# A sinkhorn attention and FFN kernel on one core: half-width FFN1 tiles taken in pairs, and new orders for the five engine queues

## The chip, the core and the metric

The kernel runs on one core of a Trainium2 chip. The metric is the device time of one execution in microseconds (us); the figure for a kernel is the median of several runs. The core has a matrix engine (PE; its weight loads are listed apart as PEld), a vector engine (DVE), a scalar engine (ACT), a general engine (POOL) and SP, which here does nothing but issue transfers. Each engine works through a queue of its own in order, and waits on semaphores for what other engines and transfers deliver. PSUM, where PE leaves its sums, has eight banks of 2 KB a partition.

## The reference

An attention in blocks, whose output goes through a two-layer feed-forward network (FFN):

```python
# q, k, v: (4 batches, 8 heads, 768 tokens, 64); sort_net: (4, 8, 8, 8); n_blocks 8, block 96
P = sort_net
for _ in range(5):
    P = P - np.max(P, axis=-1, keepdims=True)
    P = np.exp(P)
    P = P / (np.sum(P, axis=-1, keepdims=True) + 1e-09)
    P = P / (np.sum(P, axis=-2, keepdims=True) + 1e-09)
k_sorted = np.einsum('bhij,bhjcd->bhicd', P, k_b)      # blocks of keys, mixed by P
v_sorted = np.einsum('bhij,bhjcd->bhicd', P, v_b)
scores = scale * np.matmul(q_b, k_sb.transpose(0, 1, 2, 4, 3))
attn = softmax(scores)
x = (attn @ v_sb), heads joined: (3072 tokens, 512)
h = x @ w_in                                           # 512 -> 2048
g = np.maximum(h, 0.0) + alpha * np.minimum(h, 0.0)
out = g @ w_out                                        # 2048 -> 512
```

## The kernel before

**The work.** There are 4 batches (here 0 to 3) of 8 blocks, so 32 groups of 96 tokens, numbered 0 to 31; a group is one block of one batch with all its heads. For each group `attention` multiplies Q and sorted K (L758 and L762 for the row maxima and, for batch 0, L778 and L789 once more with the maximum taken off), takes the maximum on DVE (L770), the exponential on ACT (L797, L809), multiplies with the sorted values (L820, the sum of a row among its columns), divides (L825, L828) and turns the result so that features lie on the partitions (`xT`; by PE at L842 for batches 0 and 1, by a DMA transpose at L835 later). From batch 1 on (the code's `far`) the exponentials `Esb` are themselves turned by a DMA transpose that SP issues (L802, `ET`), and so are Q's rows (`turn_q`, L441: `QN` to `QT`).

The FFN takes `xT` in chunks of tokens. The first two chunks have 192 tokens (two groups each), the other seven 384. `ffn1` (L852) makes one tile, 128 of the 2048 hidden features of one chunk: four matmuls (L861) into one PSUM bank, a Relu of the negative on ACT into one of three buffers `t1` (L868), and one step on DVE (L871) that multiplies it by 1 - alpha and adds h from the bank: the leaky Relu, written to `hT`. There are 16 tiles a chunk: 32 of 192 tokens, 112 of 384. `ffn2` (L882) makes 128 tokens of the output from `hT` and `w_out`: 16 matmuls in four quarters (L895), a copy to a staging buffer (L904, done by the helper of L397) and a store that SP issues (L906). The last 128 tokens are made in two halves.

**Before the FFN.** The loads go through POOL: q, k and v of batch 0; `w_in` in four quarters (L933); the keys `KS` (L457, by `load_k`), queries `QN` (L430, by `load_q`, one load a head, eight a batch) and values `VST` (L475, by `load_v`) of batches 1 to 3; `w_out` in two halves (L938). Meanwhile DVE and ACT run the five sinkhorn rounds on a 32 x 64 matrix, `spread0` (L577) spreads P of batch 0 over the partitions, and `prep_q` (L640), `prep_k0` (L657) and `prep_v` (L721) turn and sort Q, K and V of batch 0 on PE. Until `w_out` is loaded its memory holds three selection matrices that L577 reads; the load of `w_out`'s first half must wait for L577. For later batches POOL copies keys and values into zero-padded blocks (`conv_k`, L676, to `KSz`; `conv_v`, to `VDz`; the memsets of L496 and L502 clear such blocks), and PE sorts them against `BDM` and `BDV` (`prep_k` L688, `prep_v` L716); DVE or ACT copy the results out of PSUM (L397) to `KT` and `VS`.

**What sets the order.** Every step is a node of a graph (`_Graph`), added with what it reads and writes. A table `ORDER` gives, for each of the five queues, the numbers of the nodes in the order in which that engine runs them; a number is a node's place in the order of creation, so that the same step has another number when nodes are added or dropped ahead of it. A node that may run on ACT or DVE (`EITHER`: copies from PSUM) runs on the one whose row holds it. An entry with a point, as `12.1`, is a filler: 12 matmuls of the identity into bank 1 (L1018), whose result nobody reads. A string `BANKS` gives the PSUM banks. `place` adds the waits for a bank's earlier holder, and `emit` puts semaphore waits where a node needs something of another engine or of a transfer. The durations and priorities that the nodes carry (`dur`, `prio`) are not used for the order, which is the table's alone:

```python
for x in order[e].split():
    if "." in x:
        k, b = x.split(".")
        op = _Op(("pe",), filler(int(k), int(b)), 0, 0, None, len(self.ops))
...
    else:
        op = self.ops[int(x)]
    op.eng, op.pos = e, len(row)
    row.append(op)
```

PE's first entry is a burst of 180 small matmuls (L917). A load or a transpose counts as issued when its engine has handed it over; its landing is a semaphore of its own.

Of the kernel before, what the change touches and what calls it, by code (L numbers as in the profile page):

```python
# [7 lines left out]
AP = bass.AP  # L8
# [9 lines left out]
DFF = 2048  # L18
# [4 lines left out]
XR = 1536  # L23
# [19 lines left out]
        733 675 673 904 905 909 935 910 934 801 800 831 771 772""",  # L43
    "sync": """
# [3 lines left out]
        1137 1109 1077 1065 1117 1212 1167 1191 1245 1233 1239 1251""",  # L48
    "pe": """
# [17 lines left out]
        1242 1231 1243 1246 1236 1237 1247 1248 1249""",  # L67
    "act": """
# [989 lines left out]
```

## Time and profile before

| | |
|---|---|
| median of 3 runs | 235.33 us (235.2 to 235.4) |
| the profiled execution | 234.94 us |
| its span (first to last instruction) | 233.2 us |
| PE busy | 222.9 us, 96% |
| DVE, ACT, POOL busy | 172.1, 156.4, 104.3 us |
| granted PE clock | 1.00 |
| moved by DMA | 28.99 MB, mean 124 GB/s |
| FFN1 on PE (L861) | 576 matmuls, 96.0 us |
| FFN2 on PE (L895) | 89.6 us in the 375 records that the trace holds |

All views come from one profiled execution. A group of instructions has the columns line, engine, operation, output <- inputs with their shape, count, then after the bar the busy time in us, the mean of one in ns, and the engine's idle time just before them with what ended most of it. In the view of waits a row names who waited, for what it waited, the idle us, the count and the longest. In the timeline a row has the start, the duration, the engine, the line, output <- inputs and how many instructions it holds. The windows view has a row for each stretch: start, end and length, then the busy time and count of each engine in the order PE, PEld, DVE, ACT, POOL, the granted clock, the mean share of the 16 DMA engines that is busy (over 1 where more than 16 transfers' worth overlaps) and GB/s. A DMA row gives the queue, the count, the KB of one and the us from issue to landing. Some matmul records can be missing from a trace.

### The profile page before, as it was taken

What the parts mean: (1) busy time and instruction counts of PE and PEld (TensorE: products, weight loads), DVE (VectorE), ACT (ScalarE), POOL (GpSimd) and SP (SyncE); (2) the same over time, 40 slices, a digit from 0 to 9 for tenths busy, and PEclk for the clock granted to TensorE, in tenths of its full rate; (3) what the DMA queues carried; (4) which work ended last, traced back from release to release, by engine and by line L of the source; (5) the groups of instructions that cost most, each with busy time, mean ns of one, the idle gap of its engine ahead of it and who ended that gap; (6) DMA issues with size and microseconds to landing.
All of it is one profiled execution on the core that took longest, in us unless ns stands there. A gap on an engine that the chain in (4) does not pass through costs nothing.

```text
span 233.2 us, 6024 instructions
## 1 busy us (share of the span) xinstructions
PE 222.9 (96%) x2389; PEld 143.2 (61%) x2414; DVE 172.1 (74%) x353; ACT 156.4 (67%) x431; POOL 104.3 (45%) x148
## 2 busy tenths in 40 slices
PE   7679899999999999999999999999999999999995
PEld 4369787776566666665656656556565556555553
DVE  6776889898889878988798687956769368644650
ACT  5316789878598979797858787568847864341711
POOL 7904949998999996268499570000000000000000
PEclk9999999999999999999999999999999999999999
DMA  5999999999997999996697935565481534201113
GB/s 83 220 208 210 214 191 191 218 138 140 100 109 126 154 96 170 176 195 76 131 151 83 87 67 111 129 155 148 26 214 34 70 72 143 61 0 45 45 48 135
DMA packets 63036, 28.99 MB, mean 124 GB/s; under 512 B 55312, under 2 KB 58144, under 8 KB 63008
## 3 DMA queue, kind: packets, MB, share of 16 engines
q0 software_dynamic: 23680, 13.63, 43.6%
q1 hardware_dynamic: 39328, 14.97, 32.2%
q8 instruction: 19, 0.31, 0.6%
q14 instruction: 9, 0.07, 0.1%
HBM read 27.28 MB, written 6.29 MB: 144 GB/s over the span
## 4 chain that ended last, share of the span: by engine, by line
PE 86%; DVE 8%; ACT 3%; issue 2%; POOL 0%; POOLq 0%
PE ps L895 34%; PE ps L861 34%; PE ps L758 4%; PE ps L820 3%; PE ps L721 3%; PE ps L716 2%; DVE hT L871 2%; PE ps L688 2%; PE ps L789 1%; PE ps L842 1%; DVE nm L770 1%; PE ps L778 1%; PE ps L762 1%; ACT ET L809 1%; ACT t L868 1%
## 5 line engine op out<-in xcount | busy, mean ns | idle before, releaser
L871 DVE SCALAR_TENSOR_TENSOR hT<-t,omaT,ps 128x384 bf16<-128x384 f32 (+1 forms) x144 | 76.9, 561 | 29.5 <-ACT t L868 28.6
L861 PE MATMUL ps<-xT,w_in_bf 128*128 128x384 bf16 (+1 forms) x576 | 96.0, 308 | 0.0
L895 PE MATMUL ps<-w_out_bf,hT 128*128 128x512 bf16 (+1 forms) x375 | 89.6, 370 | 1.3
L868 ACT ACTIVATE t<-ps 128x384 f32<-128x384 f32 (+1 forms) x144 | 61.3, 456 | 39.0 <-PE ps L861 29.6
L861 PEld LDWEIGHTS ps<-xT,w_in_bf 128*128 128x128 bf16 x576 | 51.9, 98 | 29.1 <-DVE hT L871 0.8
L895 PEld LDWEIGHTS ps<-w_out_bf,hT 128*128 128x128 bf16 x400 | 37.2, 98 | 31.8
L797 ACT ACTIVATE Esb<-ps,nf 96x96 bf16<-96x96 f32 x192 | 46.3, 346 | 4.9 <-DVE nf L770 4.9
L397 POOL COPY VDz<-VST 64x384 bf16<-64x384 bf16 x40 | 33.9, 848 | 7.4 <-PE ps L716 5.0
L676 POOL COPY KSz<-KS 64x512 bf16<-64x512 bf16 x36 | 22.2, 618 | 14.5 <-DMA KS<-in_k_dram 9.4
L770 DVE TENSOR_REDUCE nf<-ps 96x8 f32<-96x768 f32 x24 | 22.7, 947 | 4.0 <-PE ps L758 2.1
L828 DVE TENSOR_TENSOR xq<-ps,rec 96x512 bf16<-96x512 f32 x32 | 21.7, 682 | 0.6
L430 POOL DMA_DIRECT2D QN<-in_q_dram x24 | 20.1, 841 | 4.3 <-DVE hT L871 4.3
L397 ACT ACTIVATE KT<-ps 64x512 bf16<-64x512 f32 (+1 forms) x28 | 16.5, 589 | 6.0 <-PE ps L657 3.3
L397 ACT ACTIVATE VS<-ps 112x512 bf16<-112x512 f32 (+1 forms) x20 | 13.8, 691 | 4.6 <-PE ps L721 4.1
L397 ACT ACTIVATE outstg<-ps 128x512 f32<-128x512 f32 (+1 forms) x13 | 7.5, 580 | 10.0 <-PE ps L895 10.0
L820 PEld LDWEIGHTS ps<-VS,ET 112*128 112x128 bf16 (+1 forms) x256 | 11.1, 98 | 3.8 <-DVE hT L871 0.9
L820 PE MATMUL ps<-VS,ET 112*128 112x65 bf16 (+1 forms) x256 | 13.0, 194 | 0.2 <-DVE hT L871 0.2
L397 DVE COPY outstg<-ps 128x512 f32<-128x512 f32 (+1 forms) x12 | 7.9, 662 | 6.8 <-PE ps L895 6.8
L758 PE MATMUL ps<-KT,QT 128*96 128x192 bf16 x96 | 12.0, 247 | 0.4 <-DVE hT L871 0.4
L758 PEld LDWEIGHTS ps<-KT,QT 128*96 128x96 bf16 x96 | 9.2, 123 | 3.6 <-ACT VS L397 0.9
L825 DVE RECIPROCAL rec<-ps 96x8 f32<-96x8 f32 x32 | 6.3, 199 | 6.4 <-PE ps L820 6.2
L716 PEld LDWEIGHTS ps<-BDV,VDz 128*128 128x128 bf16 x192 | 8.4, 98 | 3.3 <-DVE VS L397 0.4
(96 smaller groups left out, 181.7 us busy)
## 6 DMA issues: line engine op xcount, KB each, us to landing
out_dram<-outstg SPq DMA_DIRECT2D x23, 256.0 KB, 2.4
KS<-in_k_dram POOLq DMA_DIRECT2D x3, 768.0 KB, 12.3
QN<-in_q_dram POOLq DMA_DIRECT2D x24, 96.0 KB, 3.9
w_in_bf<-in_moe_w_in_dram POOLq DMA_DIRECT2D x4, 512.0 KB, 11.5
w_out_bf<-in_moe_w_out_dram POOLq DMA_DIRECT2D x2, 1024.0 KB, 10.8
VST<-in_v_dram POOLq DMA_DIRECT2D x4, 384.0 KB, 8.3
hT<-in_q_dram POOLq DMA_DIRECT2D x1, 768.0 KB, 7.0
hT<-in_v_dram POOLq DMA_DIRECT2D x2, 384.0 KB, 10.4
```

Of the source, the lines that this page charges most:

```text
L397: return e.activation(o, i, ACTF.Copy) if e is nc.scalar else e.tensor_copy(o, i)
L430: G.add(POOL, lambda e, h=h: e.dma_start(AP(QN[b % 2], h % 4 * 128 + h // 4 * 64, [[3072, 128], [512, 6], [1, 64]]), AP(q.tensor, b * HB + ...
L676: G.add(POOL, lambda e, hp=hp: e.tensor_copy(AP(KSz, hp * 64 * 3072 + u % 3 * 1024 + hp * 64, [[3072, 64], [128, 8], [1, 64]]), AP(KS[n], ...
L758: inst = e.matmul(sc(2 * h4, 96, 192), AP(QT[n], h4 * 768 + i * 96, [[3072, 128], [1, 96]]), AP(KT[n], (h4 * 8 + i) * bk, [[LK, 128], [1, ...
L770: G.add(DVE, lambda e: e.tensor_reduce(AP(nx, 0, [[8, 96], [4, 2], [1, 4]]), AP(ps, X.at(), [[LP, 96], [X.step, 2], [96, 4], [1, 96]]), Ax ...
L797: inst = e.activation(AP(Esb[me], p * 128, [[1024, 96], [64, 2], [1, 48]]), AP(ps, X.at((p % 4) * 96) + p // 4 * X.step, [[LP, 96], [48, 2 ...
L820: inst = e.matmul(AP(ps, Z.at(h4 * 68) + hp * Z.step, [[LP, 128], [1, 65]]), AP(ET[et], pos(h4, hp) * 96, [[800, nk], [1, 128]]), AP(VS[n] ...
L828: G.add(DVE, lambda e: e.tensor_tensor(out=AP(xq[me], 0, [[512, 96], [256, 2], [64, 4], [1, 64]]), in0=AP(ps, Z.at(), [[LP, 96], [Z.step, ...
L861: inst = e.matmul(AP(ps, T.at(), [[LP, 128], [1, n]]), AP(w_in_bf, kt * DFF + ft * 128, [[KT_TILES * DFF, 128], [1, 128]]), AP(xT, kt * XR ...
L868: G.add(ACT, lambda e: e.activation(AP(t1[tb], 0, [[384, 128], [1, n]]), AP(ps, T.at(), [[LP, 128], [1, n]]), ACTF.Relu, scale=-1.0), t_ac ...
L871: op = G.add(DVE, lambda e: e.scalar_tensor_tensor(out=AP(hT, ft * RING + tok % RING, [[FT_TILES * RING, 128], [1, n]]), in0=AP(t1[tb], 0, ...
L895: inst = e.matmul(AP(ps, T.at(), [[LP, 128], [1, n]]), AP(hT, ft * RING + tok % RING, [[FT_TILES * RING, 128], [1, 128]]), AP(w_out_bf, ft ...
```

## The change

**Pairs.** For a chunk of 192 tokens `ffn1` now makes two tiles in one call (`nf1` is 2; for 384 tokens it is 1 and all stays as it was). The two groups of four matmuls write the two halves of one bank, one Relu covers both (384 columns), and two steps on DVE follow, one for each tile. Sixteen Relu of 384 columns stand where 32 of 192 stood, and the 32 tiles take 16 turns in the banks and the buffers `t1`.

**Order.** The tables are new: all five rows of `ORDER` and `BANKS`. Since 16 nodes are gone, numbers behind them mean other steps than before. In PE's row the first filler has 13 matmuls for 12. Copies of the `EITHER` kind change sides: of the copies to `VS` ACT has 11 for 20, of those to `xT` 10 for 6, of those to `outstg` 10 for 13, and DVE the rest.

**A duration.** The time that the graph notes for one copy to a selection matrix (L538) is 770 for 300.

The line numbers of the changed kernel are up to 6 higher from `ffn1` on: L865 stands for L861, L873 for L868, L877 for L871, L901 for L895, L939 and L944 for L933 and L938, L1024 for L1018.

```diff
@@ ORDER: one row of numbers an engine, all five written anew; of pe and sync the first line
     "pe": """
-        3 12.1 94 88 90 10.3 83 82 2.3 108 92 84 102 104 96 100 110 98 112 120 114 147 124 106 134 126 122
+        3 13.1 92 96 88 10.3 84 83 134 82 2.3 104 100 108 98 94 102 90 110 124 114 126 147 106 120 116 122
...
     "sync": """
-        0 1 177 178 179 435 451 481 182 388 180 283 181 511 567 541 577 441 457 487 614 423 686 517 645 699
+        0 1 177 178 179 181 419 435 465 372 180 407 275 182 495 525 561 551 598 425 441 471 629 683 710 745
...
 BANKS = (
-    "0203122064745001311164754230145455670137262367704236276745051102707411343436752216253562311174065672"
+    "0570250215760763253245466012345676670127013460154534270675073434463436212122747030112117432675640016"
...
@@ consts, L538
         G.add(ACT, lambda e: copy(e, AP(w_out_bf, 2048, [[WR, 32], [8, 8], [129, 8], [64, 2]]),
-                                  AP(identf, 0, [[128, 32], [1, 8], [0, 8], [0, 2]])), 300,
+                                  AP(identf, 0, [[128, 32], [1, 8], [0, 8], [0, 2]])), 770,
               r=["identf"], w=[("sel0", 2)], prio=-66.5)
@@ ffn1, L852
     def ffn1(ga, gb, ft, prio):
+
         tok, n = ga * BLK, (gb - ga) * BLK
+        nf1 = 384 // n
+        if ft % nf1:
+            return
         tb = step[0] % 3
         step[0] += 1
         T = G.bank(1, "F")
-
-        def f(e):
-            inst = None
-            for kt in range(KT_TILES):
-                inst = e.matmul(AP(ps, T.at(), [[LP, 128], [1, n]]),
-                                AP(w_in_bf, kt * DFF + ft * 128, [[KT_TILES * DFF, 128], [1, 128]]),
-                                AP(xT, kt * XR + tok % XR, [[KT_TILES * XR, 128], [1, n]]),
-                                start=(kt == 0), stop=(kt == KT_TILES - 1))
-            return inst
-        G.add(PE, f, 4 * (n / 2.4 + 2.8), r=[("xT", g % 16) for g in range(ga, gb)] + [("w_in", kt) for kt in range(KT_TILES)],
-              w=[T], prio=prio, kind="f1")
-        G.add(ACT, lambda e: e.activation(AP(t1[tb], 0, [[384, 128], [1, n]]),
-                                          AP(ps, T.at(), [[LP, 128], [1, n]]), ACTF.Relu, scale=-1.0),
-              t_act(n), r=[T], w=[("t1", tb)], prio=prio)
-        op = G.add(DVE, lambda e: e.scalar_tensor_tensor(
-            out=AP(hT, ft * RING + tok % RING, [[FT_TILES * RING, 128], [1, n]]),
-            in0=AP(t1[tb], 0, [[384, 128], [1, n]]), scalar=AP(omaT, ft, [[16, 128], [1, 1]]),
-            in1=AP(ps, T.at(), [[LP, 128], [1, n]]), op0=AluOpType.mult, op1=AluOpType.add),
-            t_dve(n) + 52, r=[T, ("t1", tb), "omaT"],
-            w=[("hT", ft, x % (RING // 64)) for x in range(tok // 64, (tok + n) // 64)], prio=prio)
-        if ga < 8 and 8 <= ft < 12:
-            op.deps.update(turned)
+        for y in range(nf1):
+            def f(e, y=y):
+                inst = None
+                for kt in range(KT_TILES):
+                    inst = e.matmul(AP(ps, T.at(y * n), [[LP, 128], [1, n]]),
+                                    AP(w_in_bf, kt * DFF + (ft + y) * 128, [[KT_TILES * DFF, 128], [1, 128]]),
+                                    AP(xT, kt * XR + tok % XR, [[KT_TILES * XR, 128], [1, n]]),
+                                    start=(kt == 0), stop=(kt == KT_TILES - 1))
+                return inst
+            G.add(PE, f, 4 * (n / 2.4 + 2.8),
+                  r=[("xT", g % 16) for g in range(ga, gb)] + [("w_in", kt) for kt in range(KT_TILES)],
+                  w=[T], prio=prio, kind="f1")
+        G.add(ACT, lambda e: e.activation(AP(t1[tb], 0, [[384, 128], [1, 384]]),
+                                          AP(ps, T.at(), [[LP, 128], [1, 384]]), ACTF.Relu, scale=-1.0),
+              t_act(384), r=[T], w=[("t1", tb)], prio=prio)
+        for y in range(nf1):
+            op = G.add(DVE, lambda e, y=y: e.scalar_tensor_tensor(
+                out=AP(hT, (ft + y) * RING + tok % RING, [[FT_TILES * RING, 128], [1, n]]),
+                in0=AP(t1[tb], y * n, [[384, 128], [1, n]]), scalar=AP(omaT, ft + y, [[16, 128], [1, 1]]),
+                in1=AP(ps, T.at(y * n), [[LP, 128], [1, n]]), op0=AluOpType.mult, op1=AluOpType.add),
+                t_dve(n) + 52, r=[T, ("t1", tb), "omaT"],
+                w=[("hT", ft + y, x % (RING // 64)) for x in range(tok // 64, (tok + n) // 64)], prio=prio)
+            if ga < 8 and 8 <= ft + y < 12:
+                op.deps.update(turned)

```

More of the change, by code (lines that the diff above doesn't have):

```diff
@@ L37 @@
     "pool": """
[5 rows of a table removed]
-        733 675 673 904 905 909 935 910 934 801 800 831 771 772""",
[5 rows of a table added]
+        894 919 889 784 918 888 661 656 785 756 755 658 816""",
     "sync": """
[3 rows of a table removed]
-        1137 1109 1077 1065 1117 1212 1167 1191 1245 1233 1239 1251""",
[3 rows of a table added]
+        1101 1130 1121 1075 1032 1196 1151 1175 1217 1229 1223 1235""",
     "pe": """
[17 rows of a table removed]
-        1242 1231 1243 1246 1236 1237 1247 1248 1249""",
-    "act": """
[10 rows of a table removed]
-        1172 1169 1181 1184 1199 1196 1178 1166 1193 1205 1214 1202 1217 1220 1223 1226 1244 1238""",
-    "dve": """
[14 rows of a table removed]
-        1224 1227 1221 1190 1232 1250""",
[17 rows of a table added]
+        1225 1226 1220 1227 1221 1232 1233""",
+    "act": """
[10 rows of a table added]
+        1222""",
+    "dve": """
[14 rows of a table added]
+        1166 1181 1211 1199 1190 1208 1205 1234""",
 }
 BANKS = (
-    "0203122064745001311164754230145455670137262367704236276745051102707411343436752216253562311174065672"
-    "3477201676743346740702564527713223344730553445231760715667072521121247054267343642003367561402412011"
-    "1762567127026304501144371767346735320234010230516701155277670130764572456713621232357500673415232367"
-    "44342340167740012315405011266062323764572732547670675251746715340"
+    "0570250215760763253245466012345676670127013460154534270675073434463436212122747030112117432675640016"
+    "7457545667273704450111730134456051301356670025023423127242016711077347014563464230120672501017644256"
+    "7012253756014530326310013452560734454460151234467730623456601326767053354556724767013231456010727001"
+    "5612743561272055612446337263471475204110274637065"
 )
```

94 rows, old and new, of the table ORDER are left out of this document.

## The prediction

> **What bounds the kernel now.** I read the page first, then PE's waits, then the busy time by stages that I cut where the waits showed a change, and last the DMA issues around two landings.
>
> ```profile
> span 233.2 us, 6024 instructions
> PE 222.9 (96%) x2389; PEld 143.2 (61%) x2414; DVE 172.1 (74%) x353; ACT 156.4 (67%) x431; POOL 104.3 (45%) x148
> ```
>
> PE is busy for all but 10.3 us. The stages (start:end, length, then busy time of PE, PEld, DVE, ACT, POOL, the granted clock, DMA share, GB/s) show where those 10.3 us are:
>
> ```profile
> 0.00:8.31 8.31, 5.22 (x193) 2.81 (x193) 5.40 (x28) 3.34 (x8) 6.97 (x14) 1.00 0.69 122
> 8.31:16.80 8.49, 7.08 (x212) 4.88 (x213) 6.16 (x24) 2.57 (x7) 2.77 (x4) 1.00 1.07 217
> 16.80:30.85 14.05, 13.40 (x243) 12.34 (x243) 10.40 (x19) 9.73 (x17) 9.29 (x14) 1.00 1.05 213
> 30.85:41.63 10.78, 9.96 (x165) 8.70 (x162) 10.27 (x28) 9.43 (x26) 7.82 (x14) 1.00 1.31 187
> 41.63:61.45 19.82, 19.19 (x247) 13.76 (x251) 17.40 (x40) 15.69 (x34) 18.07 (x25) 1.00 1.28 160
> 61.45:230.30 168.85, 167.79 (x1336) 100.70 (x1356) 122.02 (x216) 115.62 (x341) 59.37 (x80) 1.00 0.64 104
> 230.30:233.20 2.90, 0.27 (x3) 0.00 (x0) 0.43 (x1) 0.00 (x0) 0.00 (x0) 1.00 0.37 136
> ```
>
> From 61.45 on PE idles 168.85 - 167.79 = 1.06 us in 169, and PE's row of FFN2 (L895, quoted below) has 343 matmuls and 1.3 us of idle before them, where with the 32 half-wide ones there should be 400: 25 records are missing, each leaves a false gap, and these are nearly all of that 1.06. So from 61.45 to the last matmul nothing is left to gain, whatever the order. The tail (2.90 us: last copy, last store) hangs on the last half tile, which the change leaves. PE's clock is 1.00 throughout. What an order can win lies before 61.45, and PE idles there 3.09 + 1.41 + 0.65 + 0.82 + 0.63 = 6.60 us:
>
> ```profile
> PE ps L640 <- DMA hT<-in_q_dram: 1.8, 1, 1.8
> PE ps L577 <- DVE Pb L568: 0.7, 1, 0.7
> PE ps L758 <- DVE hT L871: 0.4, 1, 0.4
> ```
>
> The first of these is the landing of q, the second ends the sinkhorn chain: both precede everything and stay. That leaves about 2 us within reach (0.65 + 0.82 + 0.63).
>
> **The loads before 61.45.** The DMA share is over 1 from 8.31 to 61.45. Issue times on POOL and SP:
>
> ```profile
> 21.08 1.07 POOL L933 DMA_DIRECT2D w_in_bf<-in_moe_w_in_dram  x2
> 35.01 0.87 POOL L938 DMA_DIRECT2D w_out_bf<-in_moe_w_out_dram  x1
> 35.87 0.56 POOL L457 DMA_DIRECT2D KS<-in_k_dram  x1
> 50.91 0.85 POOL L430 DMA_DIRECT2D QN<-in_q_dram  x1
> 54.01 0.53 POOL L475 DMA_DIRECT2D VST<-in_v_dram  x1
> 54.05 5.32 SPq L441 DMA_TRANSPOSE QT<-QN  x3
> ```
>
> and, from the DMA view of short stretches, how long the last one of each of these rows (of QT the first) took from issue to landing, in the same order:
>
> ```profile
> w_in_bf<-in_moe_w_in_dram POOLq DMA_DIRECT2D x1, 512.0 KB, 9.0
> ...
> w_out_bf<-in_moe_w_out_dram POOLq DMA_DIRECT2D x1, 1024.0 KB, 10.6
> ...
> KS<-in_k_dram POOLq DMA_DIRECT2D x1, 768.0 KB, 14.7
> ...
> QN<-in_q_dram POOLq DMA_DIRECT2D x1, 96.0 KB, 3.1
> ...
> VST<-in_v_dram POOLq DMA_DIRECT2D x1, 384.0 KB, 6.7
> ...
> QT<-QN SPq DMA_TRANSPOSE x1, 7.3
> ```
>
> So the last quarter of w_in lands at 21.6 + 9.0 = 30.6, the second half of w_out at 45.6, KS of batch 2 at 50.6, the last QN of batch 1 at 54.0, VST of batch 2 at 60.7 and the first QT at 61.3. They land in the order of their issue and back to back: loads form one line. FFN1 can't begin before 30.6 (it began at 30.85). The scores of batch 1 (L758, first at 61.45) can't begin before QT, 61.3. That one start had a second master:
>
> ```profile
> 57.58 1.29 DVE VS L397 x2
> ...
> 60.23 1.15 DVE hT L871 x2
> ...
> 61.45 0.50 PE ps L758 x4
> 61.95 0.65 PE ps L861 x4
> 62.60 0.86 PE ps L895 x4
> ```
>
> On the chain of waits DVE ran 3.8 us into that start, freeing its banks at 61.38, 0.07 us after QT. Both have to come earlier for batch 1 to start earlier.
>
> **The change: tiles in pairs.** Rows of both widths, and of the fillers:
>
> ```profile
> L868 ACT ACTIVATE t<-ps 128x384 f32<-128x384 f32 x112 | 51.7, 492 | 35.5 <-PE ps L861 27.2 <-DVE hT L871 7.3
> L868 ACT ACTIVATE t<-ps 128x192 f32<-128x192 f32 x32 | 9.5, 328 | 3.4 <-PE ps L861 2.4 <-DVE hT L871 0.8
> L895 PE MATMUL ps<-w_out_bf,hT 128*128 128x512 bf16 x343 | 86.4, 379 | 1.3
> L1018 PE MATMUL ps<-identb 128*128 128x512 bf16 x24 | 6.5, 419 | 0.3 <-ACT identb L397 0.3
> ```
>
> 32 Relu of 328 ns become 16 of 492: 10.5 - 7.9 = 2.6 us less on ACT, all between 30.85 and 61.45. ACT idles (10.78 - 9.43) + (19.82 - 15.69) = 5.5 us there, so I cost this at nothing directly. PE's and DVE's instructions stay the same. Against it: the first tile of a pair now waits for the second one's four matmuls (a third of a us, half the 0.65 us of a 384 tile) and for 0.16 us more of Relu, so its hT is 0.5 us later; queued behind are FFN2's first quarters. Cover is the other pair in flight (three t buffers, eight banks); where it fails, 0.5 us once.
>
> **The order around FFN1's start.** On PE, FFN1 is `w_in_bf` (x4 one tile of 192 tokens), L842 transposes an attention output, L820 is attention times values, L688 prepares batch 1's keys. Before:
>
> ```order
> L861 MATMUL ps<-xT,w_in_bf 128x192 x4
> L842 MATMUL ps<-identb,xq 128x96 x4
> L861 MATMUL ps<-xT,w_in_bf 128x192 x8
> L820 MATMUL ps<-VS,ET 128x65 x8
> L861 MATMUL ps<-xT,w_in_bf 128x192 x20
> L688 MATMUL ps<-BDM,KSz 128x64 x8
> ```
>
> and now, from the same first FFN1 tile:
>
> ```order
> L865 MATMUL ps<-xT,w_in_bf 128x192 x8
> L842 MATMUL ps<-identb,xq 128x96 x4
> L820 MATMUL ps<-VS,ET 128x65 x8
> L865 MATMUL ps<-xT,w_in_bf 128x192 x16
> L842 MATMUL ps<-identb,xq 128x96 x4
> L865 MATMUL ps<-xT,w_in_bf 128x192 x8
> ```
>
> The same work stands before FFN1 in both, but for one more filler (6.5 / 24 = 0.27 us), which falls into the 1.8 us wait for q. FFN1 still needs the last quarter of w_in. On POOL, loads and the copies between them (`KSz`, `VDz`: blocks for batch 1) stood so:
>
> ```order
> L933 DMA w_in_bf<-in_moe_w_in_dram 128x2048
> L676 COPY KSz<-KS1 64x8x64
> L933 DMA w_in_bf<-in_moe_w_in_dram 128x2048 x2
> L475 DMA VST1<-in_v_dram 64x3072 x2
> L502 MEMSET VDz 128x1024
> L430 DMA QN1<-in_q_dram 128x6x64
> L676 COPY KSz<-KS1 64x8x64 x3
> L502 MEMSET VDz 128x1024
> L676 COPY KSz<-KS1 64x8x64
> L938 DMA w_out_bf<-in_moe_w_out_dram 128x8x512
> ```
>
> and now:
>
> ```order
> L939 DMA w_in_bf<-in_moe_w_in_dram 128x2048
> L944 DMA w_out_bf<-in_moe_w_out_dram 128x8x512
> L496 MEMSET hT 64x1536
> L676 COPY KSz<-KS1 64x8x64 x2
> L475 DMA VST1<-in_v_dram 64x3072
> L502 MEMSET VDz 128x1024
> L475 DMA VST1<-in_v_dram 64x3072
> L676 COPY KSz<-KS1 64x8x64 x2
> L944 DMA w_out_bf<-in_moe_w_out_dram 128x8x512
> ```
>
> All of w_in is issued early, but the line is the same up to it, so it lands near 30.6 and FFN1 starts near 30.85: nothing. One memset of hT now stands behind w_out's issue, which waits for the matmuls of L577:
>
> ```profile
> 9.27 1.37 POOL L496 MEMSET hT<- 64x1536 f32 x1
> ...
> 13.87 0.37 PE L577 MATMUL ps<-Pb,w_out_bf 32*128 32x8 bf16 x8
> ```
>
> Even if the last L577 ended as late as before, 14.2 + 0.9 (issue) + 1.4 = 16.5, and L721, which needs it, starts at 16.80 with the landing of v: covered, and what goes over 16.8 would cost in full. The first half of w_out comes ahead of VST: 1 MB at that stage's 187 GB/s is 5.6 us, so it lands near 36, where FFN2 first ran at 41.63. So FFN2 is free to start some 3 us earlier, and PE has something to fill the stalls of 30.85 to 61.45 with. Idle to be won there, short of the wait for L758: 0.82 + 0.63 - 0.42 = 1.03 us. I take it between 0 and all, about half.
>
> **The start of batch 1.** FFN2 is `w_out_bf`, L716 prepares values, L758 is the scores. Before:
>
> ```order
> L861 MATMUL ps<-xT,w_in_bf 128x192 x8
> L716 MATMUL ps<-BDV,VDz 128x64 x16
> L861 MATMUL ps<-xT,w_in_bf 128x384 x8
> L716 MATMUL ps<-BDV,VDz 128x64 x8
> L895 MATMUL ps<-w_out_bf,hT 128x512 x8
> L758 MATMUL ps<-KT,QT 96x192 x4
> ```
>
> and now:
>
> ```order
> L865 MATMUL ps<-xT,w_in_bf 128x384 x4
> L901 MATMUL ps<-w_out_bf,hT 128x512 x4
> L865 MATMUL ps<-xT,w_in_bf 128x384 x8
> L901 MATMUL ps<-w_out_bf,hT 128x512 x4
> L716 MATMUL ps<-BDV,VDz 128x64 x16
> L758 MATMUL ps<-KT,QT 96x192 x4
> ```
>
> Between FFN1's start and this L758 PE's row holds the same instructions in both, but three tiles of 384 tokens instead of two: 0.65 us (row 61.95) more done by then. DVE's row up to the copies that free this L758's banks no longer includes the three 384-wide hT steps (they follow), so DVE's chain ends clearly before 61.3. PE arrived at 61.45 - 0.42 = 61.03; now at 61.03 + 0.65 - (0 to 1.03) = 60.65 to 61.68. QT holds it to 61.4: the same bytes stand in line ahead (KS of batch 2 has gone behind five QN, three QN behind it, the sum stays), so the last QN lands near 54.0 and QT near 61.3. L758 starts at 61.4 to 61.7 with 0.65 us more behind it: the gain is 0.65 + 61.45 - 61.4..61.7 = 0.4 to 0.7. I take 0.6.
>
> **The sum.** ACT 0, filler 0, FFN1's start 0, batch 1's start -0.6, the rest 0: the profiled execution's 234.94 us (span 233.2 and 1.7 around it) becomes 234.3. It stands 0.4 under the median of the runs, 235.33; from that, 234.7.
>
> **Rivals.** Two more transposes, issue and time to landing, and the first L820 of batch 1:
>
> ```profile
> 71.68 1.27 SPq L441 DMA_TRANSPOSE QT<-QN  x1
> ...
> QT<-QN SPq DMA_TRANSPOSE x1, 2.5
> ...
> 65.12 6.51 SPq L802 DMA_TRANSPOSE ET<-Esb  x3
> ...
> ET<-Esb SPq DMA_TRANSPOSE x1, 6.0
> ...
> 72.24 0.41 PE L820 MATMUL ps<-VS,ET 112*128 112x65 bf16 x8
> ```
>
> *QT comes through the loads.* If transposes didn't queue behind loads, QT would be there when PE is, at 60.65 at best: gain 0.65 + 0.80 = 1.45, 233.9. For it: the QT issued at 71.68, with less load beside it, took 2.5 us. Against: this one took 7.3 and landed 0.6 after the last VST. The Trainium skill (DMA: Bandwidth & Descriptors, "Queues, rings and completion order") says that each DMA engine goes round the queues that have work, a packet at a time; by that QT would not be held until the loads are through, and the sum would be this rival's. The trace leans the other way, 61.3 after 60.7. Chance 0.1.
>
> *The gain is eaten by a wait right behind.* The first ET of batch 1 landed at 65.12 + 6.0 = 71.1, 9.7 us after its scores; L820, which needs it, came 10.8 us after them. L820 now stands closer: between the two PE has 6 FFN1 tiles and 4 quarters of FFN2 instead of 10 and 3, so 4 x 0.65 - 0.86 = 1.7 us less (one L716 more takes back some 0.2), and 9.1 to 9.3 remain. If ET still takes 9.7, PE waits 0.4 to 0.6; or the pairs' later hT costs one 0.5. Either leaves 0 to 0.2 of the gain: 235.2. Against it: QN loads of batch 2, which ran beside that ET, are issued later now. Chance 0.2.
>
> *QT comes later: slower.* POOL has to issue KS of batch 2 from behind more copies that wait for PE, and SP sends four QT in a row instead of three into the VST loads. Any gap in the line of loads moves QT by as much. The point is QT at 62.0 (61.3 + 0.65): beyond it each us is lost. A gap of 1.4, a quarter of KS's 5 us in the line, makes L758 start at 62.8: 0.7 lost, 236.0. Against: KS was issued at 35.9 for a turn that began at 45.6, and five QN issues of 0.85 us more ahead of it don't use up those 10 us. Chance 0.15.
>
> **How the numbers follow.** Forecast 0.55 (234.6 to 234.9), QT early 0.1, eaten 0.2, QT late 0.15. A measurement of this kernel tells 0.2% (0.47 us) from no change: the forecast's 0.4 to 0.7 is over that in three quarters. Faster 0.55 x 0.75 + 0.1 = 0.51; slower 0.15 and a fifth of the eaten case, 0.19; within 0.30. The range takes in QT early (233.9) and most of QT late (235.9).
>
> **What would show it.** Right: PE's idle from 30.85 to the first L758 shrinks, FFN2 starts before 40, the first L758 starts at 61.4 to 61.7 and just after QT lands, and from there to the last matmul PE takes 168.85 - 0.65 = 168.2 us. Wrong: L758 before 61 or after 62, FFN1's start off 30.85 by over 0.5, an idle of over 0.3 us before L820 near 71, or waits beyond 75.

## The result, and the profile after

| | before | after |
|---|---|---|
| median | 235.59 us (22 runs) | 234.59 us (22 runs, 233.03 to 236.69) |
| ratio | | 0.9939, interval 0.9918 to 0.9960 |
| profiled execution | 234.94 us | 233.06 us |
| its span | 233.2 us | 231.1 us |
| FFN1 starts | 30.85 | 30.10 |
| first FFN2 | 41.63 | 37.52 |
| first QT of batch 1 lands | 61.3 | 59.1 |
| first scores of batch 1 (L758) | 61.45 | 60.05 |

The change makes the kernel faster: 1.0 us between the medians, 1.4 us by the ratio, against the 0.6 that was forecast. The profiled execution of after is one of its fastest runs, 1.5 us under the median, so what it shows is the good case; a run near the median is shown below. Ratios leave out runs that lie over 1.5% above the fastest of their kernel, and since in the two kernels that delay VST the wait itself makes such runs, the median of all runs is given first for these.

The page of after, and its stages cut at the same events as those of before (first FFN1, first FFN2, first scores of batch 1, last matmul; start:end, length, then busy time of PE, PEld, DVE, ACT and POOL, the granted clock, DMA share, GB/s):

```profile
PE 223.7 (97%) x2415; PEld 143.1 (62%) x2415; DVE 176.4 (76%) x358; ACT 152.3 (66%) x410; POOL 104.0 (45%) x148
```

```profile
16.50:30.10 13.60, 13.04 (x241) 11.99 (x240) 12.59 (x23) 8.26 (x15) 7.24 (x11) 1.00 1.06 204
30.10:37.52 7.42, 7.42 (x124) 7.32 (x125) 6.96 (x23) 6.38 (x14) 5.63 (x10) 1.00 1.16 209
37.52:60.05 22.53, 21.79 (x296) 15.67 (x293) 20.19 (x43) 18.70 (x32) 20.04 (x28) 1.00 1.38 175
60.05:228.18 168.13, 168.13 (x1358) 99.96 (x1354) 125.59 (x224) 113.35 (x336) 59.36 (x80) 1.00 0.66 104
228.18:231.10 2.92, 0.27 (x3) 0.00 (x0) 0.42 (x1) 0.03 (x1) 0.00 (x0) 1.00 0.45 159
```

The span is 2.1 us shorter. The first scores start 1.40 us earlier, and from there to the last matmul PE takes 168.13 us for 168.85: one more FFN1 tile (0.65 us) is done by then. The tail is the same. The 1.40 us come from FFN1's start (0.75 us earlier) and from the stretch behind it, 29.95 us for 30.60 although it holds the further tile. Ahead of FFN1, 0.5 of the 0.75 is in part the run's luck: L721 starts with the landing of v, at 16.3 for 16.8, and over the 13 profiles here v landed between 16.1 and 16.6 in the changed kernel and its variants, and between 16.3 and 16.7 in the kernel before and its two. Where v landed alike, at 16.3 in a variant of the kernel before and at 16.4 in one of the changed kernel, FFN1 started at 30.46 and 30.18: by these two, some 0.3 us are left for the new order.

Two landings moved that the prediction took as fixed. Issue times of after, from the timeline, and from the DMA view the us from issue to landing of the same four (w_in's last quarter, the two VST of batch 2, the first QT):

```profile
10.19 0.53 POOL L939 DMA_DIRECT2D w_in_bf<-in_moe_w_in_dram  x1
47.93 0.54 POOL L475 DMA_DIRECT2D VST<-in_v_dram  x1
51.99 0.53 POOL L475 DMA_DIRECT2D VST<-in_v_dram  x1
54.04 6.25 SPq L441 DMA_TRANSPOSE QT<-QN  x4
```

```profile
w_in_bf<-in_moe_w_in_dram POOLq DMA_DIRECT2D x1, 512.0 KB, 19.5
...
VST<-in_v_dram POOLq DMA_DIRECT2D x1, 384.0 KB, 7.6
...
VST<-in_v_dram POOLq DMA_DIRECT2D x1, 384.0 KB, 6.5
...
QT<-QN SPq DMA_TRANSPOSE x1, 5.0
```

The last quarter of w_in lands at 29.7 where it landed at 30.6. VST lands at 55.5 and 58.5 (57.4 and 60.7 before), and QT, issued at 54.04 (54.05 before), lands 0.6 us behind it, at 59.1. Why VST could be earlier is seen in the same 2 us of both kernels, first before, then after:

```profile
52.00:54.00 2.00, 2.00 (x31) 1.25 (x30) 1.74 (x5) 1.68 (x6) 1.95 (x3) 1.00 1.02 75
```

```profile
52.00:54.00 2.00, 2.00 (x32) 1.52 (x30) 1.57 (x6) 0.89 (x2) 1.74 (x4) 1.00 1.35 208
```

Before, the line of loads moved 75 GB/s there: only the small packets of the last QN were left in it, and VST was issued at 52.4 and 54.0. A DMA share over 1 had hidden that. After, VST stood in line in time, and 208 GB/s went through.

With QT at 59.1 something else holds the first scores, in the timeline of after:

```profile
56.09 1.61 DVE L397 COPY VDz<-VST 64x384 bf16<-64x384 bf16 x1
56.09 1.37 POOL L669 MEMSET KT<- 64x1536 f32 x1
...
59.80 0.41 PE L716 MATMUL ps<-BDV,VDz 128*128 128x64 bf16 x8 [0.74 <-DVE hT L877]
60.05 0.51 PE L758 MATMUL ps<-KT,QT 128*96 128x192 bf16 x4
```

PE waits 0.74 us for DVE just ahead of L758, and DVE had lost about 1 us in one copy that took 1.61 us beside a memset of POOL (0.52 elsewhere).

### The profile page after: what moved, and what is told of

It is laid out like the page before. It is cut to its first block, busy times and chain, and to the rows that moved or that the text cites. A ratio compares the mean times of both kernels' runs of the same rounds, so it can differ in the third digit from the quotient of the medians.

```text
span 231.1 us, 6037 instructions
## 1 busy us (share of the span) xinstructions
PE 223.7 (97%) x2415; PEld 143.1 (62%) x2415; DVE 176.4 (76%) x358; ACT 152.3 (66%) x410; POOL 104.0 (45%) x148
## 4 chain that ended last, share of the span: by engine, by line
PE 90%; DVE 7%; ACT 1%; DMA 1%; issue 1%
PE ps L865 35%; PE ps L901 35%; PE ps L820 4%; PE ps L758 3%; PE ps L721 3%; PE ps L716 2%; PE ps L688 2%; PE ps L789 2%; PE ps L842 1%; PE ps L762 1%; PE ps L778 1%; DMA P<-in_sort_net_dram 1%; DVE VDz L397 1%; PE ps L657 1%; DVE KT L397 1%; DVE VS L397 1%
## 5 line engine op out<-in xcount | busy, mean ns | idle before, releaser
L865 PE MATMUL ps<-xT,w_in_bf 128*128 128x384 bf16 (+1 forms) x576 | 96.4, 309 | 0.2 <-ACT xT L397 0.2
L901 PE MATMUL ps<-w_out_bf,hT 128*128 128x512 bf16 (+1 forms) x400 | 93.6, 371 | 0.0
L877 DVE SCALAR_TENSOR_TENSOR hT<-t,omaT,ps 128x384 bf16<-128x384 f32 (+1 forms) x144 | 76.3, 561 | 18.3 <-ACT t L873 17.4
L873 ACT ACTIVATE t<-ps 128x384 f32<-128x384 f32 x128 | 59.6, 491 | 38.7 <-PE ps L865 25.6
L865 PEld LDWEIGHTS ps<-xT,w_in_bf 128*128 128x128 bf16 x576 | 51.3, 98 | 27.4 <-DVE hT L877 0.5
L901 PEld LDWEIGHTS ps<-w_out_bf,hT 128*128 128x128 bf16 x400 | 37.4, 98 | 32.8 <-ACT VS L397 0.4
L397 DVE CAST VS<-ps 112x512 bf16<-112x512 f32 (+1 forms) x21 | 14.4, 691 | 3.2 <-PE ps L716 3.0
L397 DVE COPY outstg<-ps 128x512 f32<-128x512 f32 (+1 forms) x15 | 10.0, 665 | 8.9 <-PE ps L901 8.9
L397 ACT ACTIVATE outstg<-ps 128x512 f32<-128x512 f32 (+1 forms) x10 | 5.7, 583 | 9.5 <-PE ps L901 8.7
L758 PE MATMUL ps<-KT,QT 128*96 128x192 bf16 x96 | 11.8, 247 | 0.0
L758 PEld LDWEIGHTS ps<-KT,QT 128*96 128x96 bf16 x96 | 9.3, 123 | 3.3 <-DVE hT L877 0.3
```

Source lines behind the costliest of these rows:

```text
L397: return e.activation(o, i, ACTF.Copy) if e is nc.scalar else e.tensor_copy(o, i)
L758: inst = e.matmul(sc(2 * h4, 96, 192), AP(QT[n], h4 * 768 + i * 96, [[3072, 128], [1, 96]]), AP(KT[n], (h4 * 8 + i) * bk, [[LK, 128], [1, ...
L865: inst = e.matmul(AP(ps, T.at(y * n), [[LP, 128], [1, n]]), AP(w_in_bf, kt * DFF + (ft + y) * 128, [[KT_TILES * DFF, 128], [1, 128]]), AP( ...
L873: G.add(ACT, lambda e: e.activation(AP(t1[tb], 0, [[384, 128], [1, 384]]), AP(ps, T.at(), [[LP, 128], [1, 384]]), ACTF.Relu, scale=-1.0), ...
L877: op = G.add(DVE, lambda e, y=y: e.scalar_tensor_tensor(out=AP(hT, (ft + y) * RING + tok % RING, [[FT_TILES * RING, 128], [1, n]]), in0=AP ...
L901: inst = e.matmul(AP(ps, T.at(), [[LP, 128], [1, n]]), AP(hT, ft * RING + tok % RING, [[FT_TILES * RING, 128], [1, 128]]), AP(w_out_bf, ft ...
```

## The experiments

Two theories were set against each other. **Of the loads**: QT lands when the loads issued ahead of it are through, and the new order of the loads makes the gain. **Of the engines**: the pairs and the new order on PE, ACT and DVE make it, and the loads don't matter. All kernels were timed beside the kernel before; ratios are to that. Edits are moves within a row of ORDER; numbers are those of the table.

**The filler back to 12.**

```diff
-        3 13.1 92 96 88
+        3 12.1 92 96 88
```

> The changed kernel with the first filler of PE back at 12 matmuls: nothing else differs, so this is also a second look at the changed kernel. Both theories expect no difference: the filler falls into the wait for q. Ratio to the kernel before 0.992 to 0.996, about 234.0 to 234.8 us. From its profile: if the times of the changed kernel differ from run to run by when the loads land (theory of the loads), then a run near 234.6 has its first QT of batch 1 about 1.5 us later than the 59.1 of the profile shown, the first scores of batch 1 waiting for it, and the landings before it late too; if they differ by something else (theory of the engines), QT lands near 59.1 again and the first scores stand near 60.05.

Median 234.40 us, ratio 0.9949 (0.9925 to 0.9973): no difference from the changed kernel. Its profile, of 234.24 us, lies near the median, and its first scores stand at 60.01, QT at 58.1. So what parts these two runs isn't the loads before 60; the theory of the loads missed here. This one has two waits of PE that after's profile doesn't have:

```profile
PE ps L820 <- DMA ET<-Esb: 0.4, 1, 0.4
...
PE ps L865 <- ACT outstg L397: 0.3, 1, 0.3
```

The first is at 149.6, the second at 186.1; they are 0.7 of the 1.2 us by which this span is longer than after's, and the rest shows as no wait. A transposed Esb that lands late is the prediction's second rival, not near 71 but later, and not in each run.

**VST of batch 2 late again.**

```diff
 pool: ... 138 143 297 141
-      400 296 351 355 399 576 387
+      296 351 355 576 400 387 399
       24 35 25 391
```

> The changed kernel with only the two loads of VST of batch 2 put back on POOL's row to where the kernel before issued them, near 52.3 and 54 us (now 47.9 and 52.0). Theory of the loads (the transposes QT land when the loads issued ahead of them are through, so that these two loads moved QT from 61.3 to 59.1): VST lands at 60 to 61, QT at 60.7 to 61.4, the first scores of batch 1 behind it at 60.8 to 61.5: 0.8 to 1.4 us slower than the changed kernel's profile, ratio to before 0.996 to 1.000. Theory of the engines (the pairs and the new order on PE, ACT and DVE make the gain; the first scores wait for DVE at 59.8): no difference, ratio 0.992 to 0.996.

Median of all 13 runs 237.45 us (233.86 to 243.69); ratio 0.9987 (0.9950 to 1.0025). The profile is of a run of 241.04 us. PE's longest wait, QT's way from issue (53.64) to landing, and the stages around:

```profile
PE ps L758 <- DMA QT<-QN: 5.7, 1, 5.7
```

```profile
QT<-QN SPq DMA_TRANSPOSE x1, 11.2
```

```profile
58.00:62.00 4.00, 1.25 (x20) 0.78 (x18) 1.74 (x3) 2.20 (x5) 1.70 (x3) 1.00 0.45 50
62.00:66.00 4.00, 1.07 (x6) 0.92 (x7) 0.19 (x1) 0.00 (x0) 1.13 (x2) 0.51 1.10 129
66.00:70.00 4.00, 4.00 (x25) 2.18 (x24) 1.97 (x3) 2.51 (x10) 3.62 (x6) 0.63 0.00 0
```

The gain is gone, and seven of the 13 runs take 237 to 244 us: this goes with the loads and rules out the engines as the only cause. But QT is at 64.8, not at the 61.3 expected. In this run VST and QT, under way together, took 10.6 and 11.2 us for the 6.7 and 7.3 of the kernel before, though the DMA engines moved only 50 GB/s from 58 to 62. By the spread of the times the delay differs from run to run; the short runs have no profile. The wait costs twice: PE comes back at half the granted clock (0.51, then 0.63). The Trainium skill (TensorE: Matmul & The Clock Gate, "Part 1: The HAM clock gate") gives half the clock after an idle window of about 3.4 us; with 5.7 us of idle the trace agrees.

**The same with three QT in a row.**

```diff
 sync: 0 1 177 178 179
-      181 419 435 465 372
+      419 435 465 181 372
```

> The changed kernel with VST of batch 2 issued late, as tried already (QT landed at 64.8 then), but with three QT in a row on SP as in the kernel before and the fourth behind three ET. If the fourth transpose in the row made the loads and the transposes crawl (the rival of the prediction in which QT comes late), the first QT lands at 60.7 to 61.5, the first scores start at 60.8 to 61.6, and the median is 234.6 to 235.6. If the late VST alone does it (loads and transposes that run at the same time slow each other, however many), QT lands past 63 in many runs again, and the median is 236 or more.

Median of all 12 runs 235.33 us (233.38 to 243.45), ratio 0.9957 (0.9917 to 0.9996). From the profile, of a run of 237.19 us, QT (issued 54.01) and the wait:

```profile
QT<-QN SPq DMA_TRANSPOSE x1, 7.5
```

```profile
PE ps L758 <- DMA QT<-QN: 2.4, 1, 2.4
```

```profile
62.00:66.00 4.00, 3.78 (x16) 2.15 (x16) 2.24 (x3) 2.42 (x9) 3.62 (x6) 0.57 0.00 0
```

QT lands at 61.5, as in the kernel before, and the median is what was expected if the fourth transpose makes the crawl. But single runs still reach 243 without it, and the times of the two kernels overlap, so its share is not shown; how loads and transposes share the engines stays open. Here 2.4 us of idle were enough to bring the clock down to 0.57. The Trainium skill (TensorE: Matmul & The Clock Gate, "Part 1: The HAM clock gate") gives a longer window, about 3.4 us; the measurement decides.

**KS and VST behind the QN.**

```diff
 pool: ... 301 347 343
-      401 174 309 311 138 143 297 141 400 296 351 355 399 576 387 24 35 25 391 568 444 445 443 575
+      174 309 311 138 143 297 141 296 351 355 400 399 401 387 24 35 25 391 444 445 443 576 568 575
```

> The changed kernel with KS and both VST of batch 2 issued only behind the last QN of batch 1 (51 to 53 us; two copies to KSz of batch 2 go behind them). Theory of the loads: 3.9 us of KS no longer stand ahead of the last QN, which lands near 50, QT near 53; the first scores wait for DVE alone, at 59.8 to 60.1 in each run, and the spread between runs shrinks: 233.0 to 233.6 in most, ratio to before 0.988 to 0.992. Theory of the engines: QT earlier changes nothing, ratio 0.992 to 0.996 with the spread as it was.

Median 237.04 us, ratio 1.0056 (1.0027 to 1.0085): slower than before, a miss of the theory of the loads as it stood. From issue to landing of the first three QT (issued 49.69, 51.02 and 52.31), and of the VST that was issued at 51.88:

```profile
QT<-QN SPq DMA_TRANSPOSE x1, 2.5
...
QT<-QN SPq DMA_TRANSPOSE x1, 7.1
...
VST<-in_v_dram POOLq DMA_DIRECT2D x1, 384.0 KB, 7.3
...
QT<-QN SPq DMA_TRANSPOSE x1, 13.2
```

The first QT, with nothing under way, takes 2.5 us. The second was issued before any of these loads and yet landed at 58.1; the third only at 65.5, when KS, issued after it, was through as well (65.0). So a transpose is held by loads issued shortly *after* it too, and loads put behind the QN only hit the next transposes: group 10 waits for the third QT, then L688 for KSz:

```profile
PE ps L758 <- DMA QT<-QN: 1.8, 1, 1.8
PE ps L688 <- POOL KSz L676: 1.5, 1, 1.5
```

One thing went well. The first scores started at 59.03, a whole us earlier than in after, and the timeline shows why:

```profile
55.99 0.52 DVE L397 COPY VDz<-VST 64x384 bf16<-64x384 bf16 x1
56.22 1.61 POOL L669 MEMSET KT<- 64x1536 f32 x1
...
59.03 0.51 PE L758 MATMUL ps<-KT,QT 128*96 128x192 bf16 x4
```

The copy began 0.2 us ahead of the memset and took 0.52 us; now it was the memset that took longer (1.61 us for 1.37).

**The same, with the memset of KT moved.**

```diff
 pool: ... 355 400 399 401
-      387 24 35 25 391
+      25 387 24 35 391
```

> The run before, and besides the second memset of KT on POOL moved from 56.1 to about 53, away from the copy VDz that DVE made at the same moment in 1.61 us (0.5 to 0.8 elsewhere). If the memset slowed that copy, DVE is through some 0.9 us earlier, and the first scores start when PE arrives, at 59.1 to 59.4: 0.4 to 0.7 us less than the run before. If the copy was slow for another reason, nothing: it takes 1.6 us again. Theory of the loads: this gain comes only because QT is there. Theory of the engines: it comes in the changed kernel as well, and the loads' move adds nothing.

Median 237.67 us, ratio 1.0076 (1.0040 to 1.0112). A miss, since the other memset came to stand where the first had been:

```profile
56.38 1.37 POOL L669 MEMSET KT<- 64x1536 f32 x1
...
56.40 1.58 DVE L397 COPY VDz<-VST 64x384 bf16<-64x384 bf16 x1
```

Begun 0.02 us behind the memset, the copy takes 1.58 us again. So one keeps the other out: the copy the memset when it begins 0.2 us ahead, the memset the copy when both begin within a few hundredths of a us. In after both records begin at 56.09, and it was the copy that waited. The Trainium skill (SBUF — State Buffer, "SBUF: two separate sides") describes a port pair that DVE, in some of its modes, and GpSimd share as an exclusive lock for a whole instruction; the trace agrees, 0.52 against 1.58 to 1.61 us.

**Two Relu a pair.**

```diff
-        G.add(ACT, lambda e: e.activation(AP(t1[tb], 0, [[384, 128], [1, 384]]),
-                                          AP(ps, T.at(), [[LP, 128], [1, 384]]), ACTF.Relu, scale=-1.0),
+        for y in range(nf1):
+            G.add(ACT, lambda e, y=y: e.activation(AP(t1[tb], y * n, [[384, 128], [1, n]]),
+                                                   AP(ps, T.at(y * n), [[LP, 128], [1, n]]), ACTF.Relu, scale=-1.0),
```

> The changed kernel with two Relu of 192 columns a pair in place of one of 384 (the shared bank, the order and all else stay). ACT has 16 x (2 x 328 - 492) ns = 2.6 us more between 30 and 55 us, where it idles some 4 us. Theory of the loads (the first scores of batch 1 hang on QT and on DVE's chain from 56 us on): 0 to 0.3 us slower than the changed kernel, ratio to before 0.992 to 0.997, the first scores at 60.0 to 60.4. Theory of the engines (the pairs carry the gain): 0.7 us slower or more, ratio 0.997 to 1.0, the first scores past 60.7.

Median 234.94 us, ratio 0.9967 (0.9945 to 0.9989). The first scores:

```profile
60.42 0.51 PE L758 MATMUL ps<-KT,QT 128*96 128x192 bf16 x4
```

They are 0.37 us later than in after, of which FFN1's start (30.18) has 0.08. Relu for Relu the pairs thus bring about 0.3 us in these two profiles, not nothing; the ratios differ by 0.2% to 0.3%, but their intervals overlap, so the times alone don't show it. The bank was still shared, so this doesn't undo the pairs as a whole; tiles with a bank each, in this order, weren't tried.

**The first half of w_out behind VST of batch 1.**

```diff
 pool: ... 17 15 131
-      132 16 251 244 145 18 146 246
+      16 251 244 145 18 146 132 246
```

> The changed kernel with the first half of w_out issued behind both VST of batch 1 on POOL's row, as in the kernel before. If the load right behind w_in decides when its last quarter lands, that goes from 29.7 to some 30.6 and FFN1 starts at 30.9 for 30.1; if not, FFN1 starts at 30.1 still. w_out's first half lands near 39.5 for 35.6, so the first FFN2, which stands at 37.5, waits some 2 us. Theory of the loads: the first scores at 61.3 to 62.2, 1.2 to 2 us slower than the changed kernel, ratio to before 0.998 to 1.003. Theory of the engines: the waits before 60 are filled from elsewhere, under 0.7 us slower, ratio under 0.998.

Median 236.62 us, ratio 1.0030 (1.0003 to 1.0057). Landing of the last quarter of w_in (issued 10.20), then FFN1's and FFN2's first matmuls and the first scores on PE:

```profile
w_in_bf<-in_moe_w_in_dram POOLq DMA_DIRECT2D x1, 512.0 KB, 20.4
```

```profile
30.71 0.82 PE L865 MATMUL ps<-xT,w_in_bf 128*128 128x192 bf16 x8 [0.60 <-ACT xT L397]
...
39.42 0.81 PE L901 MATMUL ps<-w_out_bf,hT 128*128 128x512 bf16 x3 [1.15 <-DMA w_out_bf<-in_moe_w_out_dram]
...
61.70 0.51 PE L758 MATMUL ps<-KT,QT 128*96 128x192 bf16 x4
```

This one move costs 0.9%, some 2 us, more than the whole gain. w_in's last quarter lands at 30.6 as in the kernel before: the load behind it in the line decides; why is not shown. In the four profiles in which VST follows w_in (the kernel before and its two variants below, and this one) it lands at 30.4 to 30.9 and FFN1 starts at 30.46 to 31.03; in all nine others, in which w_out follows, it lands at 29.7 to 30.1 and FFN1 starts at 29.99 to 30.41. Here PE stands ready for 0.60 us; the view names xT, which ended at 30.23, but the wait went on to 30.71, so w_in is what ended it. The rest is FFN2's 1.15 us.

**The loads of VST alone, in the kernel before, with a memset moved.**

```diff
 pool: ... 321 261
-      25 142 144 365 143 585 416 357 415 403
+      142 144 143 416 415 365 585 357 25 403
```

> The kernel before with the loads alone as the change has them at this place: the last three QN of batch 1 close up and both VST of batch 2 are issued right behind them, at 49.6 to 51 us (before 52.4 and 54.0); one memset of KT goes behind two copies. VST lands at 57 to 58.5, QT at 58 to 59 for 61.3. The first scores of batch 1 still wait for DVE's chain, which ends at 61.38: they start at 61.3 to 61.5 and the time is the kernel before's, ratio 0.998 to 1.001 (theory of the loads with DVE as the second master, as forecast). If QT alone held them, they start when PE arrives, near 61.0, and the ratio is 0.996 to 0.998. Theory of the engines: ratio 1.000, with QT early and without effect.

Median 237.35 us, ratio 1.0076 (1.0049 to 1.0103): a miss by the edit itself. QT did land early, at 59.6, but two of DVE's copies took 1.28 and 1.57 us, one beside a copy of POOL, the other beside the memset of KT, and PE then waited 1.27 us for DVE at 55.95:

```profile
50.80 1.28 DVE L397 COPY VDz<-VST 64x384 bf16<-64x384 bf16 x1
50.83 0.86 POOL L397 COPY VDz<-VST 64x384 bf16<-64x384 bf16 x1
...
53.53 1.37 POOL L669 MEMSET KT<- 64x1536 f32 x1
53.57 1.57 DVE L397 COPY VDz<-VST 64x384 bf16<-64x384 bf16 x1
```

**The loads of VST alone, the memsets left where they were.**

```diff
 pool: ... 25 142 144 365 143
-      585 416 357 415 403
+      416 415 585 357 403
```

> The kernel before with nothing but the two VST of batch 2 moved up to stand right behind the last QN (51.8 and 52.3 us, before 52.4 and 54.0); two copies on POOL come half a us later, the memsets of KT stay. Theory of the loads, with DVE as the second master: VST lands at 57.5 to 59.5, QT at 59 to 60.4 for 61.3, the first scores still start at 61.3 to 61.6 behind DVE, ratio 0.999 to 1.001. If QT alone held the first scores they start at 61.0 and the ratio is 0.997 to 0.999. If the issue of VST doesn't decide when QT lands, QT stays at 61.3.

Median 235.18 us, ratio 0.9986 (0.9949 to 1.0023), which can't be told from before. In its profile FFN1 starts 0.39 us earlier than in that of before. QT (issued 53.97), the first scores on PE, and DVE's two steps ahead of them:

```profile
QT<-QN SPq DMA_TRANSPOSE x1, 6.6
```

```profile
60.73 0.50 PE L758 MATMUL ps<-KT,QT 128*96 128x192 bf16 x4 [0.18 <-ACT VS L397]
```

```profile
59.76 1.14 DVE L871 SCALAR_TENSOR_TENSOR hT<-t,omaT,ps 128x384 bf16<-128x384 f32 x2
```

L758 starts at 60.73 while DVE is in these two steps until 60.90. In the kernel before they ended at 61.38, just ahead of L758, and the waits named them. They can't have held it: nothing that L758 needs is in them. QT held it, in both kernels 0.14 us after its landing (61.31 to 61.45, 60.59 to 60.73). The copy to VS that the view names here was done at 60.64, just behind QT; in the kernel before it was done at 61.11, 0.2 us ahead of QT. PE's idle ahead of L758 shrinks from 0.42 to 0.18 us: the loads alone were worth a quarter of a us there. PE itself came 0.48 us earlier, 0.39 of it since FFN1's start.

**The memset of KT alone, and with both VST in a row, in the changed kernel.**

```diff
 pool, memset alone: ... 141 400 296
-      351 355 399 576 387 24 35 25 391
+      25 351 355 399 576 387 24 35 391
 pool, both: ... 141 400
-      296 351 355 399 576 387 24 35 25 391
+      399 296 25 351 355 576 387 24 35 391
```

> The changed kernel with only the second memset of KT moved ahead of the copy that waits for PE (49.2 for 56.1 us); both VST of batch 2 are issued as in the changed kernel. It parts the two moves of the run that did both. Theory of the memset (POOL's memset kept DVE's copy VDz waiting at 56.1): the copy takes 0.5 to 0.6, DVE is through near 58.8, and the first scores start at the later of PE's arrival (59.1) and QT (58.1 to 59.1 in the changed kernel's profiles, and later in some runs): 59.1 to 59.5, ratio to before 0.989 to 0.993. Theory of the loads alone (the second VST issued earlier made that run's gain): the ratio stays at the changed kernel's, 0.993 to 0.996.

> The changed kernel with two moves on POOL's row: the second VST of batch 2 issued right behind the first (48.5 for 52.0 us), and the second memset of KT ahead of a copy that waits for PE (49.2 for 56.1 us), so that it can't stand in the way of DVE's copy VDz at 56.1 (1.61 us beside the memset, 0.52 where the copy began first, in the runs so far). Theory of the loads: the copy takes 0.5 to 0.8, DVE is through near 58.9, QT is there at 57.5 to 58.5, and the first scores start when PE arrives, at 59.0 to 59.3 for 60.05: 0.7 to 1.0 us less than the changed kernel, ratio to before 0.988 to 0.992. If QT lands no earlier than 59.1, 0.5 to 0.7 less. If the memset wasn't the cause, no gain.

The memset alone: median 233.73 us, ratio 0.9918 (0.9884 to 0.9952). Both: median 233.22 us (232.49 to 233.79), ratio 0.9901 (0.9877 to 0.9925), the lowest here, though of 6 runs and with intervals that overlap; the profiles carry the argument. Copy and first scores, memset alone, then both:

```profile
56.08 0.52 DVE L397 COPY VDz<-VST 64x384 bf16<-64x384 bf16 x1
...
59.43 0.50 PE L758 MATMUL ps<-KT,QT 128*96 128x192 bf16 x4
```

```profile
56.06 0.54 DVE L397 COPY VDz<-VST 64x384 bf16<-64x384 bf16 x1
...
59.11 0.51 PE L758 MATMUL ps<-KT,QT 128*96 128x192 bf16 x4
```

With DVE out of the way the first scores hang on QT again: with the memset alone it lands at 59.29, and L758 follows 0.14 us later. With VST earlier QT lands at 58.1, and L758 starts when PE arrives. Both theories were thus half of it: loads and DVE take turns as the last.

## Why the prediction was right in the whole, and where it failed

- **Right: the forecast of a gain, its place and the further tile.** The first scores of batch 1 decide, one more tile is done by then, the stage behind takes 168.13 us (168.2 forecast), and no wait comes near 71. The predicted 234.7 us and the measured median agree, but that is partly luck: the gain was undersized, 0.6 forecast and 1.0 to 1.4 measured, and two of the prediction's own signs of being wrong came true, L758 before 61 (60.05) and FFN1's start off by over 0.5 (0.75).
- **Wrong: "the same bytes stand in line ahead", so QT near 61.3.** The last QN did land at 54.0 as forecast. But the loads were not back to back: at 52 to 54 the line carried 75 GB/s. VST, issued earlier, filled it and brought QT forward by 2.2 us. The gain by the ratio, 1.4 us, has the size that the first rival (QT early) gave, but not its mechanism: QT did not come through the loads, as the VST delayed in the changed kernel showed: with it QT came at 61.5 and 64.8.
- **Wrong: "That one start had a second master".** DVE's end at 61.38 was a coincidence. QT held L758, so the order on DVE did not have to change for that, only QT and PE had to come earlier. In the changed kernel DVE did become the last, by a copy kept out by a memset, which no term held.
- **Wrong: "so it lands near 30.6 and FFN1 starts near 30.85: nothing".** w_in landed at 29.7, and FFN1 started 0.75 us earlier. In the kernel before PE was busy right up to FFN1, so w_in did not hold it; but PE came earlier now (v's landing, shorter waits), and a landing at 30.6 would have stopped it, as the kernel with w_out behind VST shows (30.71). The premise that only what stands ahead in the line counts is what failed; the load behind counts too.
- **Too small: w_out's early half.** It was given a share of 1.03 us; moved back alone it costs some 2, of which 0.6 lie in w_in's landing and 1.15 in FFN2's wait.
- **Between FFN1's start and the scores** the forecast took half of 1.03 us of idle. Visible idle there fell from 1.45 us (0.2 to 0.3 of it false gaps of missing records) to 0.74, all of it the new wait for DVE. The rest of the 1.3 us saved in this stretch shows as no wait: the same matmuls stand closer. Its cause stays open.
- **Pairs at nothing:** some 0.3 us on the path, by one profile of the kernel with two Relu. The 2.6 us less on ACT were too many: two Relu in a row overlap, so that the busy time of the 32 was 9.5 us before, not 10.5, and 8.4 in the kernel with two Relu, against 7.9 for the 16.
- **The rival "QT later: slower" did not come**, since both VST had been issued when the four QT began. A late QT does cost: with VST delayed by 2 to 5 us QT landed at 64.8 and the median was 237.45. But it came later than the gap in the line of loads explains. The filler cost nothing, as forecast.
- **The rival of a gain eaten by ET** holds in part: the run near the median has such a wait at 149.6, the fastest has none.

## What to carry to other kernels

A landing must be read with the rate of the stretch before it: a line of loads whose GB/s fall to a third may be running dry, however high the DMA share, and the next issue then sets the landing. What is issued and not yet landed tells that from a crawl: 75 GB/s here came of late issues, 50 GB/s with VST delayed came with VST under way. When a wait ends within 0.1 us of two events, look for a run in which they come apart before calling both masters. And a search over orders should know that a POOL memset and a DVE copy such as those here keep each other out, and that loads near a DMA transpose can cost more than their bytes.

## What the runs showed of the hardware

- A DMA transpose of QN takes 2.5 us from issue to landing alone, 3.5 to 7.5 behind loads, and up to 11.2 and 13.2 with loads issued beside it; loads issued after it hold it too. In 8 of the 11 profiles in which VST is issued before the first QT or up to 0.6 us behind it, QT lands 0.5 to 0.7 us after the second VST.
- The copy VDz on DVE takes 0.52 us alone and 1.57 to 1.61 when a memset of 1.37 us on POOL begins with it or up to 0.04 us before it; when the copy begins 0.23 us ahead, the memset takes 1.61.
- After 2.4 us of idle, up to 61.66, the granted clock was 0.57 from 62 to 66; with 5.7 us of idle, up to 64.93, it was 0.51 from 62 to 66 and 0.63 from 66 to 70. After 1.8 us of idle (KS and VST behind the QN) L758's four matmuls took 0.50 us at once, as elsewhere.
- Moving w_out's first half from behind w_in to behind VST moved the landing of w_in's last quarter from 29.7 to 30.6.
